# Float32r scores in the later batches, a short MAX8 for the 32nd score, and masks by VectorE alone

## The chip, the cores and the metric

The kernel runs on one core of a Trainium2 chip. The metric is the device time of one execution in microseconds. A core has five engines with a queue each: TensorE (PE in the profile), VectorE (DVE), ScalarE (ACT), GpSimd (POOL) and SyncE (SP, which issues the transfers between memory and on-chip memory). Each works through its queue in order; semaphores order work between them.

## The reference

Three stages follow one another. The first is attention over 4 batches of 8 heads, 576 positions, width 64, in which only the 32 largest scores of a row count:

```python
scores = scale * np.matmul(q, k.transpose(0, 1, 3, 2))
kth = np.partition(scores, -top_k, axis=-1)[..., -top_k:-top_k + 1]
mask = scores >= kth
scores = np.where(mask, scores, -1000000000.0)
scores = scores - np.max(scores, axis=-1, keepdims=True)
attn = np.exp(scores)
attn = attn / (np.sum(attn, axis=-1, keepdims=True) + 1e-09)
return np.matmul(attn, v).astype(np.float32)
```

The second is a dense layer on the 2304 tokens of width 512, `(x @ w_a) * (x @ w_b) @ w_out` with inner width 1536. The third picks one of 8 experts for each token (the largest of 8 logits) and computes `gate * relu(x @ w1[e]) @ w2[e]` with inner width 1024.

## The kernel before, in words

All work is written as operations with an engine, a planned cost, a position and the tiles that they read and write (`Plan.op`). `Plan.emit` plays the operations through a model of the engines, always taking the ready operation with the lowest position, and writes each engine's queue in the order that comes out. So a changed cost or a new operation can change the order of everything. Once written, the queues are fixed.

**Attention** works on units: a batch and a pair of heads. Batch 0 is cut into two halves by rows, so it has 8 half units (0 to 7); batches 1 to 3 have 4 whole units each (8 to 19). `load_unit` fetches k, q and v; `prep_unit` transposes k and q on TensorE into the buffer tp in PSUM (L473, L476), and ScalarE copies them out to kT and qT (L488). A unit's rows are cut into tiles of 128 rows of one head, taken in pairs of two heads ("N"), and one mixed tile of 64 rows of both heads ("M"). There are 144 tiles, 36 a batch.

For a pair, TensorE computes the scores in float32 in two halves of 288 columns (L533; the mixed tile L518). ScalarE copies them to the tile s (L537). VectorE forms, for each column and its partner in the other half, the larger (m) and the smaller (n) of the two scores (L544 and L545). Then it finds the 32nd largest: four rounds of MAX8 on m (L556, L572), which give the 32 largest of m in sorted order, with MATCH_REPLACE8 between them (L569), and one MAX8 on n (L575). `attn_kth` merges the two lists with a minimum of sorted ranks 24 to 31 against the eight of n in reverse order (L585) and a maximum (L587). After the first MAX8 GpSimd makes the negative maximum nm (L559) and ScalarE the exponentials e (L564).

`attn_out` masks a tile in one of two ways, which `masked(i)` picks by the tile's number: in batches 0 and 1 three tiles of four, in batches 2 and 3 one of three, 78 in all, take the split way. There VectorE compares s with the 32nd score (L609), GpSimd multiplies the result by e (L611), and ScalarE sums the row (L612). The other 66 take one fused VectorE instruction that compares, multiplies and sums (L615). TensorE transposes the masked tile (L640, L649; mixed L623 to L625), ScalarE copies it out (L644, L651), and TensorE multiplies by v (L661, L665). `attn_norm` divides by the sums.

**Around it.** In batch 0 the weights of the dense layer are converted: 36 pieces pass through ScalarE, VectorE (L383, L386), GpSimd (L389, L395) and back to memory. The dense layer of a batch (`moe1`: L758, and L788 for w_out) runs in float32r with each operand split into a high and a low part. Its matmuls have the lowest priority of all, so they fill TensorE between the steps of the next batch's attention. Its weights come in through a buffer of three (L736, L776) by the SP queue, as do the loads of k, q and v. After attention follow the dense layer of batch 3 and the experts (`expert`, L1033 to L1238).

The lines that carry the choice of the mask:

```python
if masked(i):
    P(DVE, c_ts(S), pos, lambda: nc.vector.tensor_scalar(am(), sc(), kth(), None, op0=OP.is_ge), ...)
    P(POOL, c_pool(S), pos, lambda: nc.gpsimd.tensor_mul(am(), am(), e()), r=[e], w=[amk])
    P(ACT, c_act(S, True) + 90, pos, lambda: nc.scalar.activation(
        e(), am(), AF.Copy, accum_out=r.sum()[:, j:j + 1]), r=[amk], w=[e, (r.sum, j)])
else:
    P(DVE, c_dve(S) + 60, pos, lambda: nc.vector.scalar_tensor_tensor(
        am(), sc(), kth(), e(), op0=OP.is_ge, op1=OP.mult, accum_out=r.sum()[:, j:j + 1]), ...)
```

## Time and profile before

| | |
|---|---|
| median of 3 runs | 1248.7 us (1246.32 to 1249.34) |
| profiled execution | 1250.73 us, its span 1248.9 us |
| mean granted TensorE clock | 0.944 |
| TensorE busy | 1136.4 us (91% of the span) |
| VectorE busy | 893.8 us (72%) |
| ScalarE busy | 741.5 us (59%) |
| GpSimd busy | 539.2 us (43%) |

The shares are means over stages that differ much: VectorE works almost without a break up to about 805 us and little after that. The end of a matmul is modelled, so a busy TensorE can still have short gaps. The first masks fall at 22 us; attention ends at about 818 us.

### The profile page before, as it was taken

To read this page: it belongs to the slowest core of one execution; us is meant where nothing else is said; L and a number is where in the kernel's file an instruction comes from. 1 tells how busy PE (TensorE), PEld (TensorE's weight loads), DVE (VectorE), ACT (ScalarE), POOL (GpSimd) and SP (SyncE) were. 2 spreads that over 40 slices of the span, in tenths; PEclk is the share of its full clock that TensorE was granted. 3 is DMA by queue.
4 is the path that set the end of the run, shared out by engine and by line. 5 is a ranking of instruction groups with operands and counts; after the bars stand their busy time and mean duration, and the time that the engine had idled before them with its cause. 6 is when DMAs were issued, how large, how long until landed. Compare 5 with 4: busy or idle time off the path is not lost.

```text
span 1248.9 us, 22260 instructions
## 1 busy us (share of the span) xinstructions
PE 1136.4 (91%) x7614; PEld 950.9 (76%) x7614; DVE 893.8 (72%) x2574; ACT 741.5 (59%) x1639; POOL 539.2 (43%) x673
## 2 busy tenths in 40 slices
PE   5666587987999999999999999999899999999997
PEld 2333365675687878878878777899899889999996
DVE  6999989999989999989999898901004644444451
ACT  6767677777677776656766665633223545544451
POOL 4766667577554744324544532555334110000011
PEclk9966588898899999999999999999999999999999
DMA  7486566898466554243243322345545645554550
GB/s 232 137 275 186 164 178 188 288 327 264 161 208 200 188 183 131 77 130 131 77 137 100 113 86 104 119 140 202 196 167 179 200 151 171 181 175 145 166 180 28
DMA packets 133375, 208.01 MB, mean 167 GB/s; under 512 B 53075, under 2 KB 95059, under 8 KB 125573
## 3 DMA queue, kind: packets, MB, share of 16 engines
q1 hardware_dynamic: 130037, 197.04, 48.5%
q0 software_dynamic: 3216, 9.46, 2.0%
q8 instruction: 62, 1.02, 0.3%
q14 instruction: 60, 0.49, 0.1%
HBM read 171.82 MB, written 35.25 MB: 166 GB/s over the span
## 4 chain that ended last, share of the span: by engine, by line
PE 62%; DVE 20%; issue 7%; DMA 5%; ACT 3%; POOL 2%; SPq 1%; POOLq 0%; ACTq 0%; DVEq 0%
PE ab L758 20%; PE ab L788 11%; PE sp L533 5%; PE ab L1116 5%; DVE m L569 4%; PE pv L661 4%; DVE kt L572 4%; PE tp L640 3%; PE ms L1165 3%; PE pv L1165 3%; DVE am L609 2%; DVE kt L556 1%; DMA xsort<-rows,pi 1%; DVE am L615 1%; DVE m L545 1%
## 5 line engine op out<-in xcount | busy, mean ns | idle before, releaser
L758 PE MATMUL ab<-xh,wt 128*128 128x320 f32 (+1 forms) x1344 | 311.1, 309 | 3.4 <-ACT sb L743 3.4
L758 PEld LDWEIGHTS ab<-xh,wt 128*128 128x128 f32 x1344 | 228.3, 192 | 30.3 <-issue 22.6
L758 PE MATMUL ab<-xl,wt 128*128 128x320 f32 (+1 forms) x672 | 200.4, 298 | 0.0
L569 DVE MATCH_REPLACE8 m<-kt,m 128x288 f32<-128x288 f32 x432 | 190.6, 447 | 0.0
L572 DVE MAX8 kt<-m 128x8 f32<-128x288 f32 x432 | 184.8, 452 | 0.7
L788 PE MATMUL ab<-gH,wt 128*128 128x320 f32 (+1 forms) x768 | 172.0, 307 | 2.8 <-DMA wt<-wos 2.8
L533 PE MATMUL sp<-kT,qT 64*128 64x288 f32 x512 | 111.2, 514 | 40.5 <-ACT s L537 13.0
L766 POOL TENSOR_TENSOR sa<-sa,sb 128x320 f32<-128x320 f32 (+1 forms) x96 | 80.2, 836 | 149.2 <-ACT sb L743 145.6
L788 PEld LDWEIGHTS ab<-gH,wt 128*128 128x128 f32 x768 | 129.8, 193 | 14.9 <-issue 10.1
L611 POOL TENSOR_TENSOR am<-am,e 128x576 f32<-128x576 f32 x78 | 119.1, 1532 | 31.8 <-DVE am L609 25.7
L758 PEld LDWEIGHTS ab<-xl,wt 128*128 128x128 f32 x672 | 129.2, 192 | 0.0
L1190 POOL DMA_INDIRECT out_dram<-y,ti x23 | 23.0, 999 | 228.0 <-ACT y L1184 213.3
L564 ACT ACTIVATE e<-s,nm 128x576 f32<-128x576 f32 x144 | 109.5, 777 | 16.4 <-POOL nm L559 15.5
L788 PE MATMUL ab<-gT,wt 128*128 128x320 f32 (+1 forms) x384 | 114.8, 299 | 0.0
L640 PE MATMUL tp<-idr,am 128*128 128x128 f32 x512 | 87.9, 307 | 24.7 <-DVE am L615 12.3
L1034 DVE TENSOR_TENSOR wp<-raw,wp 128x1024 fp32r<-128x1024 f32 (+1 forms) x73 | 67.5, 943 | 55.0 <-ACT wp L1033 52.6
L537 ACT COPY s<-sp 128x576 f32<-128x576 f32 x128 | 81.8, 639 | 41.9 <-PE sp L533 31.0
L395 POOL TENSOR_TENSOR gT<-sa,gH 128x320 fp32r<-128x320 f32 (+1 forms) x96 | 82.6, 861 | 39.5 <-ACT gH L394 38.1
L640 PEld LDWEIGHTS tp<-idr,am 128*128 128x128 f32 x512 | 65.7, 157 | 44.4 <-POOL am L611 14.4
L533 PEld LDWEIGHTS sp<-kT,qT 64*128 64x128 f32 x512 | 44.1, 209 | 72.3 <-issue 28.2
L1116 PE MATMUL ab<-xgh,wp 128*128 128x304 f32 (+6 forms) x352 | 89.5, 312 | 1.2 <-DVE gT L1123 0.7
L644 ACT COPY aT<-tp 128x512 f32<-128x512 f32 x128 | 73.4, 586 | 24.6 <-PE tp L640 23.7
(286 smaller groups left out, 2559.6 us busy)
## 6 DMA issues: line engine op xcount, KB each, us to landing
wt<-ws SPq DMA_DIRECT2D x54, 1024.0 KB, 4.8
wt<-wos SPq DMA_DIRECT2D x44, 768.0 KB, 4.6
raw<-in_moe_w_dram SPq DMA_DIRECT2D x64, 512.0 KB, 3.5
xsort<-rows SPq DMA_DIRECT2D x8, 771.0 KB, 10.5
wp<-ws SPq DMA_DIRECT2D x6, 1024.0 KB
rawk<-in_k_dram SPq DMA_DIRECT2D x40, 128.0 KB, 3.6
vt<-in_v_dram SPq DMA_DIRECT2D x20, 256.0 KB, 4.4
gT<-in_moe_w_a_dram SPq DMA_DIRECT2D x8, 512.0 KB
```

The lines of the kernel that those rows point to most:

```text
L395: P(POOL, c_pool(cost), pos, lambda: nc.gpsimd.tensor_sub(lo(), src(), fr(hi())), r=rd + wh, w=wl)
L533: res = nc.tensor.matmul(sp()[:, h, 0:HS], u.qT()[a, c * 128:(c + 1) * 128], u.kT()[a, k0 + hf * HS:k0 + (hf + 1) * HS], start=True, stop= ...
L537: P(ACT, c_act(S), pos, lambda hf=hf, sp=sp: nc.scalar.copy(s()[:, :, hf * HS:(hf + 1) * HS], sp()[:, :, 0:HS]), r=[sp], w=[(s, (h, hf)) f ...
L564: P(ACT, c_act(S, True) + 90, pos, lambda h=h, e=e: nc.scalar.activation(e(), s()[:, h], AF.Exp, bias=nm()[:, h], scale=SCALE), r=[(s, (h, ...
L569: P(DVE, c_dve(HS), pos + 5.0 * h, lambda x=x, h=h, j=j: nc.vector.match_replace(out=m()[:, h], in_to_replace=kt(j, 8 * x - 8, 8 * x), in_ ...
L572: P(DVE, c_dve(HS), pos + 5.0 * h, lambda x=x, h=h, j=j: nc.vector.max(out=kt(j, 8 * x, 8 * x + 8), in_=m()[:, h]), r=[(m, h)], w=[KT(j, x)])
L611: P(POOL, c_pool(S), pos, lambda: nc.gpsimd.tensor_mul(am(), am(), e()), r=[e], w=[amk])
L640: res = nc.tensor.transpose(tp()[:, 512 * h + x * 128:512 * h + (x + 1) * 128], z()[:, 640 * h + x * 128:640 * h + (x + 1) * 128], idf)
L758: res = nc.tensor.matmul(pa()[:, 0:n], view()[:, m, wi, ko, :], xv()[:, ko], start=(ko == 0 and x == 0), stop=(ko == KO - 1 and x == 2))
L766: P(POOL, c_pool(n), pos, lambda: nc.gpsimd.tensor_mul(sa()[:, 0:n], sa()[:, 0:n], sb()[:, 0:n]), r=[sb], w=[sa])
L788: res = nc.tensor.matmul(pa()[:, 0:n], wv()[:, wi, f, :], gv()[:, f, :], start=(f == 0 and x == 0), stop=(f == HB - 1 and x == 2))
L1116: res = nc.tensor.matmul(pa()[:, 0:cap], p1[ko]()[:, wi, f * 128:(f + 1) * 128], xv()[:, ko], start=(ko == 0 and i == 0), stop=(ko == KO - ...
```

## The change

There are four edits. Units 8 to 19 (batches 1 to 3) compute their scores in float32r: k and q are split into a high part (ScalarE) and a low part (GpSimd), laid side by side in `hl`, and transposed together, so that the contraction runs over 128 rows, high and low. A second copy of kT with the two halves of its rows swapped (kS) is made by two transfers on the SP queue, and each score half is the sum of a product with kT and one with kS. Units 0 to 7 keep the float32 way (`u.f`, the list FU). The merge of the 32nd score becomes one MAX8 over 16 numbers for each tile. `masked` is false for every tile, so all 144 take the fused instruction. In the mixed tile one transpose grows from 64 × 64 to 128 × 128, over a part of the mask buffer that is set to zero once. The planned costs of the float32 score change from 510 to 780.

```diff
+    FU = opts.get("fu", range(8))
...
-    am_t = [cst.tile([128, S], F32, name="am0")]
+    am_t = [cst.tile([128, 640], F32, name="am0")]
...
+    nc.gpsimd.memset(am_t[0][:, S:640], 0.0)
...
+    for i in range(2):
+        qm_t.append(cst.tile([128, 192], F32R, name=f"qm{i}"))
+        nc.gpsimd.memset(fr(qm_t[i]), 0.0)
...
+            load(c_dma(262144), pos, lambda z=z: z()[:, 0:8, :].rearrange("p (h c) d -> p h c d", h=2),
+                 src[b, h0:h0 + 2, 0:512, :].rearrange("h (p c) d -> p h c d", c=4), [(z, 0)])
             for h in range(2):
+                load(c_dma(16384), pos, lambda z=z, h=h: z()[64 * h:64 * h + 64, 8, :], src[b, h0 + h, 512:576, :],
+                     [(z, 1 + h)])
...
+        u.kS = T(p_at, [128, 2, 640], F32R, "kS", opts.get("kS", 2))
+        for ni, nm in enumerate(("k", "q")):
             raw = u.raw[nm]
+            p0 = pos + 3 * ni * step
+            hl = T(p_at, [128, 9, 2, 64], F32R, "hl", opts.get("hl", 1))
+            P(ACT, c_act(576, True), p0, lambda raw=raw, hl=hl: nc.scalar.copy(hl()[:, :, 0, :], raw()[:, 0:9, :]),
+              r=[raw], w=[(hl, 0)])
+            P(POOL, c_pool(576), p0, lambda raw=raw, hl=hl: nc.gpsimd.tensor_sub(
+                hl()[:, :, 1, :], raw()[:, 0:9, :], fr(hl()[:, :, 0, :])), r=[raw, (hl, 0)], w=[(hl, 1)])
+            for h in range(2):
+                p1 = p0 + step * (1 + h)
+                t = T(p_ps, [128, 1024], F32R, "tp", 1)
+                lst = [(c, 4 * h + c) for c in range(4)] + ([(4, 8)] if h else [])
+
+                def tr(t=t, lst=lst, hl=hl):
+                    for c, j in lst:
+                        r = nc.tensor.transpose(t()[:, c * 128:(c + 1) * 128],
+                                                hl()[:, j].rearrange("p a d -> p (a d)"), idr)
+                    return r
+                P(PE, 56 * len(lst), p1, tr, r=[hl], w=[t], act=0)
...
+                    for a in range(2):
+                        u.mark = P(SP, c_dma(294912), p1, lambda a=a: nc.sync.dma_start(
+                            fr(u.kS()[64 * a:64 * a + 64]).rearrange("p h c -> p (h c)")[:, 64:],
+                            fr(u.kT()[64 - 64 * a:128 - 64 * a]).rearrange("p h c -> p (h c)")[:, 64:]),
+                          r=[u.kT], w=[(u.kS, a)])
...
+                        for x, kk in enumerate((u.kT(), u.kS())):
+                            res = nc.tensor.matmul(sp()[:, h, 0:HS], u.qT()[:, h, c * 128:(c + 1) * 128], kk[:, h, kc],
+                                                   start=(x == 0), stop=(x == 1))
...
-        P(DVE, 77 + 8 * (j1 - j0 - 1), pos, lambda: nc.vector.tensor_tensor(
-            kt(32, 40), r.kt()[:, j0:j1, 30:22:-1], kt(40, 48), op=OP.min), r=KT(2) + KT(3) + KT(5), w=KT(4))
-        P(DVE, 78 + 9 * (j1 - j0 - 1), pos, lambda: nc.vector.tensor_reduce(
-            r.kth()[:, j0:j1], kt(31, 40), axis=AX.X, op=OP.max), r=KT(3) + KT(4), w=[(r.kth, j) for j in range(j0, j1)])
...
+        for j in range(j0, j1):
+            P(DVE, 80, pos, lambda j=j: nc.vector.max(out=r.kt()[:, j, 40:48], in_=r.kt()[:, j, 24:40]),
+              r=[(r.kt, (j, 3)), (r.kt, (j, 4))], w=[(r.kt, (j, 5))])
...
-                nc.tensor.transpose(tp()[0:64, 512:576], am()[0:64, 512:S], idf[0:64, 0:64])
...
+                nc.tensor.transpose(tp()[:, 512:640], amz()[:, 512:640], idf)
...
-        return any(a <= i < b and i % m < n for a, b, n, m in opts.get("mk", ((0, 72, 3, 4), (72, 144, 1, 3))))
+        return any(a <= i < b and i % m < n for a, b, n, m in opts.get("mk", ()))
```

## Rows read from the trace of the kernel before

**Rows 1.** Busy us by stretch: PE, PEld, DVE, ACT, POOL, PE clock, DMA, GB/s.

```profile
0.00:245.00 245.00, 165.92 (x781) 107.22 (x781) 229.03 (x605) 173.99 (x374) 160.51 (x177) 0.78 0.67 205
245.00:355.00 110.00, 97.02 (x607) 73.02 (x604) 104.41 (x319) 80.38 (x183) 68.27 (x75) 0.92 0.77 246
355.00:810.00 455.00, 452.61 (x3278) 365.77 (x3277) 415.15 (x1358) 304.75 (x709) 212.37 (x292) 1.00 0.39 130
810.00:1249.00 439.00, 420.89 (x2956) 404.86 (x2954) 145.18 (x296) 182.39 (x374) 98.05 (x130) 0.99 0.49 163
```

**Rows 2.** The chain that ended last, around the end of attention: start, us, what.

```profile
811.52 0.87 PE tp L640 x8
...
818.39 7.11 PE ab L758 x54
825.50 19.20 PE ab L788 x144
```

**Rows 3.** Groups by line, VectorE, 0 to 355 us: busy us, mean ns, idle before.

```profile
L609 DVE TENSOR_SCALAR am<-s,kth 128x576 f32<-128x576 f32 x42 | 29.5, 726 | 0.1
L556 DVE MAX8 kt<-m 128x8 f32<-128x288 f32 x58 | 25.7, 452 | 0.0
...
L615 DVE SCALAR_TENSOR_TENSOR am<-s,kth,e 128x576 f32<-128x576 f32 x14 | 16.9, 1209 | 0.0
...
L585 DVE TENSOR_TENSOR kt<-kt 128x16 f32<-128x16 f32 (+1 forms) x31 | 11.0, 354 | 0.1
...
L587 DVE TENSOR_REDUCE kth<-kt 128x2 f32<-128x18 f32 (+1 forms) x31 | 4.9, 159 | 0.1
...
L615 DVE DVE_READ_ACCUMULATOR am<-s,kth,e 128x1 f32 x14 | 1.1, 80 | 0.0
```

**Rows 4.** Single instructions in order of time, VectorE and GpSimd: start, us, what.

```profile
264.79 1.40 POOL L611 TENSOR_TENSOR am<-am,e 128x576 f32<-128x576 f32 x1
...
264.95 1.85 DVE L615 SCALAR_TENSOR_TENSOR am<-s,kth,e 128x576 f32<-128x576 f32 x1
...
272.08 0.42 DVE L383 TENSOR_SCALAR x<-x 128x512 int32<-128x512 int32 x1
...
273.99 0.68 DVE L386 SCALAR_TENSOR_TENSOR x<-xl,x 128x512 int32<-128x512 int32 x1
...
314.02 0.79 DVE L615 SCALAR_TENSOR_TENSOR am<-s,kth,e 128x576 f32<-128x576 f32 x1
...
314.75 0.51 DVE L609 TENSOR_SCALAR am<-s,kth 128x576 f32<-128x576 f32 x1
```

**Rows 5.** VectorE busy by stretch for L386 alone, then for L383 alone.

```profile
0.00:355.00 355.00, 38.82 (x36) 0.82 0.70 218
...
0.00:355.00 355.00, 25.51 (x36) 0.82 0.70 218
```

**Rows 6.** Groups by line, GpSimd, 0 to 355 us.

```profile
L611 POOL TENSOR_TENSOR am<-am,e 128x576 f32<-128x576 f32 x42 | 65.0, 1556 | 15.2 <-DVE am L609 15.0
```

**Rows 7.** Single instructions in order of time, TensorE, around one half score.

```profile
500.74 0.76 PE L533 MATMUL sp<-kT,qT 64*128 64x288 f32 x4
501.42 0.66 PE L640 MATMUL tp<-idr,am 128*128 128x128 f32 x4
```

**Rows 8.** Line L640: what TensorE's idle time before it waited for, us, times.

```profile
  DVE am L615: 25.9, 13
  POOL am L611: 19.5, 25
  ACT qT L488: 9.1, 6
```

**Rows 9.** Groups by line, TensorE, 355 to 810 us.

```profile
L640 PE MATMUL tp<-idr,am 128*128 128x128 f32 x308 | 45.3, 275 | 0.5 <-ACT aT L644 0.2
```

**Rows 10.** Waits of the SP queue: us in total, times, longest us.

```profile
SPq L776 <- PE ab L758: 170.2, 21, 16.2
```

**Rows 11.** Transfers by line: count, KB each, median us to landing.

```profile
vt<-in_v_dram SPq DMA_DIRECT2D x20, 256.0 KB, 4.4
```

More of the change, by code (lines that the diff above doesn't have):

```diff
@@ L323, in fused_kernel @@
         nc.gpsimd.memset(gb_t[i], 0.0)
+    QM = [P_.fixed(t) for t in qm_t]
     RR = [P_.fixed(t) for t in rr_t]
@@ L427, in load_unit @@
         u = Rec()
-        u.b, u.p, u.first = b, p, ui == 0
+        u.b, u.p, u.f, u.first = b, p, ui in FU, ui == 0
         ch = [x - x // 3 for g in groups for x in GT[g] if x != 2]
@@ new lines, in prep_unit, with tr, out @@
+        u.qm, u.rr = QM[i % 2], RR[i % len(RR)]
+        u.qT = T(p_at, [128, 2, 512], F32R, "qT", 2)
+        u.kT = T(p_at, [128, 2, 640], F32R, "kT", 2)
+        if u.f:
+            u.qv, u.kv = (lambda z=z: fr(z()).rearrange("p h c -> p (h c)")[:, 0:640] for z in (u.qT, u.kT))
+            for ni, (nm, z, dst) in enumerate((("k", u.kT, u.kv), ("q", u.qT, u.qv))):
+                raw = u.raw[nm]
+                p1 = pos + 3 * ni * step
+                a, e, last = u.c if nm == "q" else (0, 4, True)
+                t = T(p_ps, [128, 512], F32, "pv", 1) if u.first and nm == "q" else T(p_ps, [128, 1024], F32, "tp", 1)
+                cut = [(a, e, last)] if not u.first or nm == "q" else [(0, 2, False), (2, 4, True)]
+                for a, e, last in cut:
+                    o = 128 * e if u.first and nm == "q" else 512
+                    def tr(t=t, raw=raw, a=a, e=e, last=last, o=o):
+                        for c in range(a, e):
+                            res = nc.tensor.transpose(t()[:, c * 128:(c + 1) * 128],
+                                                      raw()[:, 2 * c:2 * c + 2, :].rearrange("p a d -> p (a d)"), idf)
+                        if last:
+                            res = nc.tensor.transpose(t()[:, o:o + 64], raw()[0:64, 8:10, :].rearrange("p a d -> p (a d)"),
+                                                      idf[0:64, 0:64])
+                        return res
+                    P(PE, 110 * (e - a) + 60 * last, p1, tr, r=[raw], w=[(t, a)], act=0)
+                    def out(t=t, dst=dst, a=a, e=e, last=last, o=o, f=64 * (nm == "k")):
+                        if last and f:
+                            nc.scalar.copy(dst()[:, 0:64], t()[:, 512:S])
+                        if last and 128 * e < 512:
+                            nc.scalar.copy(dst()[:, 512:S], t()[:, o:o + 64])
+                            last = False
+                        x, y = 128 * a, S if last else 128 * e
+                        return nc.scalar.copy(dst()[:, f + x:f + y], t()[:, x:y])
+                    u.mark = P(ACT, c_act(128 * (e - a) + 64 * last) + (150 if last and (e < 4 or nm == "k") else 0), p1,
+                               out, r=[(t, a)], w=[(z, a)])
+            return
@@ L495, in new_group @@
         r.kt = T(p_sml, [128, 5, 48], F32, "kt", 2)
-        r.kth = T(p_sml, [128, 5], F32, "kth", 2)
         r.sum = T(p_sml, [128, 5], F32, "sum", 2)
@@ L515, in score @@
             def score():
-                for hh, hf in ((0, 0), (1, 1), (0, 1), (1, 0)):
-                    a = slice(64 * hh, 64 * hh + 64)
-                    res = nc.tensor.matmul(sp()[a, hf, 0:HS], u.qT()[a, 512:576], u.kT()[a, 64 + hf * HS:64 + (hf + 1) * HS],
-                                           start=True, stop=True)
-                return res
-            P(PE, 980, pos, score, r=[u.qT, u.kT], w=[sp], label=f"score{u.b}")
+                if u.f:
+                    for hh, hf in ((0, 0), (1, 1), (0, 1), (1, 0)):
+                        a = slice(64 * hh, 64 * hh + 64)
+                        res = nc.tensor.matmul(sp()[a, hf, 0:HS], u.qv()[a, 512:576],
+                                               u.kv()[a, 64 + hf * HS:64 + (hf + 1) * HS], start=True, stop=True)
+                    return res
+                for hf in range(2):
+                    for hh in range(2):
+                        for kk in (u.kT(), u.kS()):
+                            res = nc.tensor.matmul(sp()[:, hf, 0:HS], u.qm()[:, 64 * hh:64 * hh + 128],
+                                                   kk[:, hh, 64 + hf * HS:64 + (hf + 1) * HS],
+                                                   start=(hh == 0 and kk is u.kT()), stop=(hh == 1 and kk is u.kS()))
+                return res
+            P(PE, 980 if u.f else c_mm(HS, 8), pos, score, r=[u.qT, u.kT] if u.f else [u.qm, u.kT, u.kS], w=[sp],
+              label=f"score{u.b}")
             P(ACT, c_act(S), pos, lambda: nc.scalar.copy(
```

92 lines of the change are left out of this document (40 added, 52 removed).

## The prediction

> **What bounds the kernel now.** I read the busy time by stretch first, then the costs of the mask and 32nd-score instructions in the first stretch, then single instructions in order of time, then what TensorE and the transfer queue wait for. The stretches [rows 1] show two regimes. Up to 355 us VectorE is busy 229.0 of 245 and 104.4 of 110 us, while TensorE has gaps and a granted clock of 0.78 and 0.92. From 355 us to the end of attention near 810 us TensorE is busy 452.6 of 455 us at clock 1.00, and it stays near full after that. So there are two prices. A microsecond that VectorE gains or loses before 355 us moves everything behind it. After 355 us the order is set by the sum of TensorE's work, because the low-priority matmuls of the dense layers fill whatever attention leaves. VectorE idles 39.8 us of that stretch, and when the last attention matmul is done 7.1 + 19.2 = 26.3 us of the older batch's filler is still to run [rows 2]. Lengthening attention there is therefore hidden up to about 26 us, while TensorE work counts in full.
>
> **VectorE in the first 355 us.** 56 tiles are masked there: 42 with the short comparison plus a GpSimd product, 14 with the fused instruction [rows 3]. The change turns the 42 into fused ones.
>
> Removed: 42 × 0.726 = 30.5 us of comparisons. Added: 42 fused instructions. The nearest row is the fused instruction of the same stretch, 1.209 us, and its accumulator read of 0.080 us: 42 × 1.289 = 54.1 us. The 31 pairs of minimum and reduction cost 11.0 + 4.9 = 15.9 us. In their place come 56 MAX8 over 16 numbers. No row shows one; it lies between the reduction over 18 numbers or fewer (0.159) and MAX8 over 288 (0.452), and I take 0.16, from the row nearest in size: 9.0 us. At 0.452 it would be 25.3 us. Without any further effect VectorE gains 54.1 − 30.5 − 15.9 + 9.0 = +16.7 us.
>
> Against this stands contention. Alone, a fused instruction takes 0.79 us and a comparison 0.51; one that starts while a GpSimd product runs took 1.85 us and ended 0.61 us after that product [rows 4]. The two conversion instructions at L386 and L383 take 38.8 and 25.5 us for 36 each [rows 5] where their undelayed rows say 0.68 and 0.42 [rows 4]: 14.3 + 10.4 = 24.7 us of delay. The products are 65.0 of GpSimd's 228.8 us in this stretch [rows 1, 6], 28%. I credit the conversion with that share, 7.0 us, and leave the fused instructions at their row, since 56 of them instead of 14 now meet the rest of GpSimd's work. That gives +9.7 us. The ends: +16.7 with no relief; and with every fused instruction at its undelayed 0.79 us, 42 × 0.87 − 30.5 − 14 × 0.419 − 6.9 − 7.0 = −13.7 us. I stay nearer the upper end because the only fused instructions measured in this stretch have that mean.
>
> The Trainium skill's page "SBUF — State Buffer", section "Who interferes with whom", says that VectorE and GpSimd share one port pair as an exclusive lock, taken by VectorE instructions with two SBUF inputs and by the two-port modes of tensor_scalar. The 1.85 us row agrees. If that is all there is to the delays, removing products removes whole blocks, and MAX8, with one input, cannot be blocked at all: the sum would move towards the −13.7 end, which the faster rival below takes from rows.
>
> After 355 us the same swap is at most 36 × (1.289 − 0.726) = 20 us; it hides in the 39.8 us that VectorE idles and in the 26.3 us of filler. If that cover were gone it would be paid.
>
> **GpSimd and ScalarE.** The products and the ScalarE sums go. Twelve later units gain two GpSimd subtractions and two ScalarE copies each for the high and low parts, and more copies out of PSUM. GpSimd was busy 212.4 and ScalarE 304.8 of 455 us, so I cost them at nothing. The fused instruction now also waits for the exponential, which a comparison did not; behind it VectorE's whole queue would stand. The exponential is issued after the first of four MAX8 rounds, so three rounds cover it.
>
> **TensorE after 355 us.** A pair's half score is four instructions of 0.68 us in all (500.74 to 501.42) [rows 7]. The float32r version is four matmuls of 288 columns. The 144 filler matmuls, half of them 320 and half 256 columns wide, take 19.20 us [rows 2], 0.133 each: 0.533 us. Eight halves a unit save 1.18 us. The mixed tile keeps eight instructions, and I leave it even. Preparing a unit now takes eight full transposes and two narrow ones; the float32r path takes 18 full ones. No row shows a float32r transpose. The nearest is the float32 one, 0.87 us for eight, 0.109 each [rows 2]: 1.96 us instead of about 0.98 (narrow ones at half). The wider mixed-tile transpose adds 0.05. Over 12 units: 12 × (−1.18 + 0.98 + 0.05) = −1.8 us. At half the price of the row it is −13.6 us, at twice +21.7 us. The sum takes −1.8.
>
> **New waits.** Preparing a unit becomes a chain: loads, ScalarE copy, GpSimd subtraction, then four trips from TensorE to ScalarE through the single buffer tp instead of two, then two copies of kT into kS on the SP queue. TensorE now waits 9.1 us in all behind the copies of the last trip (L488) [rows 8], 0.46 us for each of 20 units. Two more trips a unit and the kS transfer, in 12 units of which the first two or three lie before 355 us, give 12 × 2 × 0.46 = 11 us if nothing covers them; TensorE has filler to run between trips, and its transposes wait only 0.5 us after 355 us [rows 9], so I take 4 us. The ends are 0 and 18 us, the upper one if a third of a landing like vt's 4.4 us [rows 11] is bare in each unit. Behind a waiting kS transfer on SP stand weight loads. One of those holds the queue for 170.2 / 21 = 8.1 us on average today [rows 10], and kS can stand behind it as well.
>
> TensorE waits 19.5 us in 25 waits behind products, but 25.9 us in 13 behind fused instructions [rows 8]. I cost the removal of the first at nothing: before 355 us VectorE's queue sets the pace, and a shorter wait for GpSimd becomes a wait for VectorE.
>
> The small set-up fills on GpSimd cost nothing; it idles over a third of the first stretch.
>
> **The sum.** +9.7 − 1.8 + 4 = +11.9 us on the profiled execution's 1250.7 us (span 1248.9 and 1.8 around it): 1262.6. The median of the runs, 1248.7, is 2.0 lower, so I predict 1260.6, rounded to 1260.5.
>
> **Rivals.** *The port comes free (faster).* The delays are all blocks by GpSimd and the removed products take them along. For it: the 1.85 us row. Against: conversion work fills the room. Price: −13.7 on VectorE, other terms kept, −13.7 − 1.8 + 4 = −11.5, 1237 us. It decides once the fused instructions of the first stretch fall below 1.209 − 11.9 / 42 = 0.93 us on average. Chance 0.27. This is the way in which the lock that the Trainium skill's page "SBUF — State Buffer" describes would work here.
>
> *The terms cancel.* The relief lands about halfway, fused instructions near 0.93 us: 1249 us. Chance 0.13.
>
> *Float32r transposes cost twice the float32 row* (or kS comes late in every unit, about as dear). TensorE then has 21.7 instead of −1.8: 1284 us. For it: no row has the shape. Against: the float32r filler takes 0.133 us for 288 columns, which is 0.059 for 128. Chance 0.10.
>
> *My forecast*: 0.50, with a range of its own from 1252 to 1270 (VectorE +3 to +16.7, waits 0 to 8, rounded).
>
> The 8-in-10 range is 1237 to 1280: it leaves out half of the faster rival and most of the third. A measurement of this kernel tells 0.3%, some 3.7 us, from no change. Faster 0.27, same 0.13, slower 0.60.
>
> **What would show it.** In the profile after: the fused instruction's mean in the first stretch (1.2 us, or below 0.93); the time at which TensorE becomes full (about 10 us later than 355, or earlier); L386 and L383 delays of 18 us, not 25 or 10; the price of a float32r transpose, start to start, beside 0.109 us; TensorE's idle time before scores and transposes in the later batches; the time by which the short MAX8 differs from 0.16 us. The prediction is wrong if VectorE is done with the first 56 tiles no later than now, or if TensorE has gaps of several us a unit after 355 us.

## The result, and the profile after

| | before | after |
|---|---|---|
| median of the runs | 1247.9 us (4 runs) | 1233.4 us (1231.7 to 1235.9, 4 runs) |
| profiled execution's span | 1248.9 us | 1231.4 us |
| mean granted TensorE clock | 0.944 | 0.956 |

The ratio is 0.9882, with a 95% interval of 0.9866 to 0.9898: the changed kernel is 1.2% faster. The forecast was 1260.5 us, with a range from 1237 to 1280. Both the sign and the range were wrong.

Percentages of whole kernels below are ratios of their runs to runs of the kernel before on the same chip; 1% is 12.5 us.

The stretches of the changed kernel, in the columns of [rows 1] (the last one ends with the span, at 1231.4 us):

```profile
0.00:245.00 245.00, 169.91 (x893) 117.64 (x894) 229.22 (x660) 170.72 (x353) 137.79 (x167) 0.85 0.77 233
245.00:355.00 110.00, 98.19 (x730) 87.32 (x728) 103.65 (x331) 77.06 (x177) 57.98 (x77) 0.97 0.86 273
355.00:810.00 455.00, 433.54 (x3290) 389.31 (x3289) 419.94 (x1357) 296.97 (x690) 181.61 (x269) 0.99 0.40 130
810.00:1249.00 439.00, 401.94 (x2804) 386.92 (x2802) 143.51 (x291) 173.35 (x349) 83.17 (x110) 0.98 0.48 158
```

Two things differ from [rows 1]. TensorE does more in the first 355 us (1623 matmul records instead of 1388, at a higher granted clock). And from 355 to 810 us it is idle for 455 − 433.5 = 21.5 us, where it was 2.4 before.

VectorE's groups of the mask and of the 32nd score, 0 to 355 us, answer to [rows 3]:

```profile
L680 DVE SCALAR_TENSOR_TENSOR am<-s,kt,e 128x576 f32<-128x576 f32 x58 | 58.7, 1029 | 0.1
L652 DVE MAX8 kt<-kt 128x8 f32<-128x16 f32 x58 | 8.2, 161 | 0.0
L680 DVE DVE_READ_ACCUMULATOR am<-s,kt,e 128x1 f32 x58 | 4.5, 78 | 0.0
```

The conversion lines, L386 and L383 before and L392 and L389 now, as in [rows 5]:

```profile
0.00:355.00 355.00, 29.18 (x36) 0.88 0.80 245
...
0.00:355.00 355.00, 21.17 (x36) 0.88 0.80 245
```

The fused instruction takes 1.03 us, not 1.21. The conversion takes 50.3 us, not 64.3. For the same 56 tiles VectorE's account is: masks 56 × (1.029 + 0.078) − 42 × 0.726 − 14 × 1.289 = +13.5 us, 32nd score 9.0 − 15.9 = −6.9, conversion −14.0: in all −7.4 us. The 56th mask ends at 341.7 us, where it ended at 348.9 before, so the account holds within 1 us.

More than those 7 us is gained on TensorE. Its filler, the dense layer of batch 0, starts at 147.3 instead of 160.1 us, and by 355 us 642 of its matmuls have started, 474 before. At the 0.133 us of [rows 2] the 168 more are 22.3 us of TensorE's later work. Two things that the filler needs come sooner: attention of batch 0 (36 masks) ends at 230.1 instead of 237.9 us, and VectorE's last conversion instruction at 269 instead of 297 us. No run separates what each of them gives.

Part of it is given back around 400 to 450 us. TensorE's busy time there, its count, granted clock, DMA share and GB/s, in the kernel before:

```profile
400.00:450.00 50.00, 50.00 (x382) 1.00 0.67 228
```

and in the changed one:

```profile
400.00:450.00 50.00, 38.23 (x254) 0.90 0.34 110
```

Single instructions of the changed kernel there, in order of time, show what is missing (start, us, what, idle time before it and what ended it):

```profile
420.26 0.31 PE L824 MATMUL ab<-xl,wt 128*128 128x320 f32 x1
420.41 0.31 PE L824 MATMUL ab<-xh,wt 128*128 128x320 f32 x1
423.53 0.37 PE L601 MATMUL sp<-kT,qT 128*128 128x288 f32 x1 [2.81 <-DVE kt L652]
...
425.33 1.02 PE L706 MATMUL tp<-idr,am 128*128 128x128 f32 x4 [1.04 <-DVE am L680]
...
437.46 0.53 PE L523 MATMUL tp<-idr,hl 128*128 128x128 f32 x4 [1.97 <-POOL hl L514]
437.83 0.35 PE L824 MATMUL ab<-xh,wt 128*128 128x256 f32 x1
```

Between 420.4 and 437.8 us no filler (L824, L854) runs. The dense layer of batch 0 is used up (its 864 matmuls have started by 402.2 us). Of batch 1's, 24 matmuls of the first 320 rows run up to 420.4 us; the next in the queue have to wait for batch 1's attention, whose last mask ends at 426.0 us. In the kernel before, the filler of batch 0 lasts until attention is through, and there is no such pause.

At the end of attention, on the chain of waits, there is again filler left of the older batch, as in [rows 2]:

```profile
807.79 3.23 PE ab L854 x24
811.02 0.22 PE pv L769 x2
811.24 13.51 PE ab L854 x102
```

### The profile page after: what moved, and what is told of

Read it like the earlier page. It is cut to its first block, busy times and chain, and to the rows that moved or that the text cites. A ratio compares the mean times of both kernels' runs of the same rounds, so it can differ in the third digit from the quotient of the medians.

```text
span 1231.4 us, 22514 instructions
## 1 busy us (share of the span) xinstructions
PE 1103.6 (90%) x7710; PEld 981.2 (80%) x7710; DVE 896.3 (73%) x2636; ACT 718.1 (58%) x1567; POOL 460.6 (37%) x622
## 3 DMA queue, kind: packets, MB, share of 16 engines
q8 instruction: 63, 1.03, 0.4%
## 4 chain that ended last, share of the span: by engine, by line
PE 55%; DVE 14%; DMA 11%; issue 8%; ACT 7%; POOL 4%; SPq 1%; POOLq 0%; ACTq 0%; DVEq 0%
PE ab L824 16%; PE ab L854 9%; PE ab L1182 5%; PE pv L727 5%; DVE am L680 3%; DVE m L638 3%; PE ms L1231 3%; PE pv L1231 3%; PE sp L601 3%; DVE kt L641 2%; PE tp L706 2%; DMA xsort<-rows,pi 2%; DMA rawk<-in_k_dram 2%; DMA wt<-wos 1%; PE pv L731 1%
## 5 line engine op out<-in xcount | busy, mean ns | idle before, releaser
L824 PE MATMUL ab<-xh,wt 128*128 128x320 f32 (+1 forms) x1344 | 303.9, 304 | 3.9 <-ACT sb L809 3.8
L824 PEld LDWEIGHTS ab<-xh,wt 128*128 128x128 f32 x1344 | 227.6, 191 | 13.2 <-issue 7.8
L824 PE MATMUL ab<-xl,wt 128*128 128x320 f32 (+1 forms) x672 | 199.9, 297 | 0.0
L641 DVE MAX8 kt<-m 128x8 f32<-128x288 f32 x432 | 182.3, 444 | 0.5
L854 PE MATMUL ab<-gH,wt 128*128 128x320 f32 (+1 forms) x768 | 171.8, 305 | 4.5 <-DMA wt<-wos 4.5
L680 DVE SCALAR_TENSOR_TENSOR am<-s,kt,e 128x576 f32<-128x576 f32 x144 | 139.8, 996 | 0.3
L854 PEld LDWEIGHTS ab<-gH,wt 128*128 128x128 f32 x768 | 130.7, 193 | 6.7 <-DMA wt<-wos 3.9
L824 PEld LDWEIGHTS ab<-xl,wt 128*128 128x128 f32 x672 | 128.8, 192 | 0.0
L854 PE MATMUL ab<-gT,wt 128*128 128x320 f32 (+1 forms) x384 | 115.1, 300 | 0.0
L1100 DVE TENSOR_TENSOR wp<-raw,wp 128x1024 fp32r<-128x1024 f32 (+1 forms) x73 | 67.4, 942 | 55.6 <-ACT wp L1099 55.2
L706 PE MATMUL tp<-idr,am 128*128 128x128 f32 x512 | 84.8, 304 | 20.3 <-ACT aT L710 7.2
L401 POOL TENSOR_TENSOR gT<-sa,gH 128x320 fp32r<-128x320 f32 (+1 forms) x96 | 84.6, 881 | 45.8 <-ACT gH L400 45.4
L706 PEld LDWEIGHTS tp<-idr,am 128*128 128x128 f32 x512 | 64.1, 155 | 38.6 <-ACT aT L710 15.8
L710 ACT COPY aT<-tp 128x512 f32<-128x512 f32 x128 | 72.4, 587 | 26.6 <-PE tp L706 25.8
L727 PE MATMUL pv<-aT,vt 128*64 128x320 f32 (+1 forms) x512 | 79.2, 451 | 6.5 <-ACT aT L695 4.5
L809 ACT ACTIVATE sa<-ab 128x320 f32<-128x320 f32 (+1 forms) x120 | 49.4, 412 | 53.9 <-PE ab L824 30.7
```

The lines of the kernel that those rows point to most:

```text
L401: P(POOL, c_pool(cost), pos, lambda: nc.gpsimd.tensor_sub(lo(), src(), fr(hi())), r=rd + wh, w=wl)
L641: P(DVE, c_dve(HS), pos + 5.0 * h, lambda x=x, h=h, j=j: nc.vector.max(out=kt(j, 8 * x, 8 * x + 8), in_=m()[:, h]), r=[(m, h)], w=[KT(j, x)])
L706: res = nc.tensor.transpose(tp()[:, 512 * h + x * 128:512 * h + (x + 1) * 128], z()[:, 640 * h + x * 128:640 * h + (x + 1) * 128], idf)
L727: nc.tensor.matmul(pv()[64 * h:64 * h + 64, 0:n], u.vt()[:, h, j, :], r.aT[h]()[:, j, 0:n], start=(j == 0), stop=False)
L824: res = nc.tensor.matmul(pa()[:, 0:n], view()[:, m, wi, ko, :], xv()[:, ko], start=(ko == 0 and x == 0), stop=(ko == KO - 1 and x == 2))
L854: res = nc.tensor.matmul(pa()[:, 0:n], wv()[:, wi, f, :], gv()[:, f, :], start=(f == 0 and x == 0), stop=(f == HB - 1 and x == 2))
```

## The experiments

Theory A is that the gain comes from VectorE in the first stretch: fewer and shorter instructions there, and above all fewer that stand still while GpSimd holds the path to on-chip memory; for float32r it counts TensorE's saved work in full. Theory B is that the gain comes from TensorE's waits behind the products, theory C that it comes from the changed order of the queues. The conditions of each are in the expectations. For float32r, theory F1 is that GpSimd's subtractions delay VectorE later on, F2 that the longer preparation delays TensorE, and F3 that TensorE's saving meets a stretch without filler in batch 1. The diffs are against the kernel before where it says so, else against the changed one. After each time stands the ratio to the kernel before.

**Masks alone** (kernel before).

```diff
-        ... for a, b, n, m in opts.get("mk", ((0, 72, 3, 4), (72, 144, 1, 3))))
+        ... for a, b, n, m in opts.get("mk", ()))
```

> The kernel before with the fused mask on all 144 tiles and nothing else changed. Theory A (the GpSimd products delayed VectorE by holding what they share, and that goes): fused instructions in the first 355 us fall to 1.03 us, the conversion lines L386 and L383 lose 14 us of delay, which pays for the longer masks (42 x 0.38 = 16 us), so 1246 to 1250 us. Theory B (TensorE's waits behind products were the price, so the gain of the whole change is here): 1236 to 1240 us. Forecast on record (longer masks are paid): 1255 to 1265 us.

Measured: 1236.5 us, 0.9898 (0.9863 to 0.9933). Fused 1.040 us, conversion 45.6 us, 36th mask at 227.2 us. Against the forecast, fused instructions for every tile are by themselves worth 1%. The time lies in theory B's range; the signs on VectorE are theory A's, with 18.7 us of relief on the conversion instead of 14. This run alone does not decide between the two.

**Short MAX8 alone** (kernel before).

```diff
-        P(DVE, ..., nc.vector.tensor_tensor(kt(32, 40), r.kt()[:, j0:j1, 30:22:-1], kt(40, 48), op=OP.min), ...)
-        P(DVE, ..., nc.vector.tensor_reduce(r.kth()[:, j0:j1], kt(31, 40), axis=AX.X, op=OP.max), ...)
...
+        for j in range(j0, j1):
+            P(DVE, 80, ..., nc.vector.max(out=r.kt()[:, j, 40:48], in_=r.kt()[:, j, 24:40]), ...)
```

> The kernel before with one MAX8 over 16 numbers a tile instead of the minimum and the reduction a pair. Theory A: VectorE saves 15.9 - 9.0 = 6.9 us before 355 us and nothing counts after, so 1240 to 1243 us. Theory B: nothing, 1246 to 1250 us.

Measured: 1238.8 us, 0.9914 (0.9891 to 0.9936). MAX8 over 16 numbers takes 0.160 us. The gain is somewhat larger than theory A's; theory B, which gave it nothing, falls here. The conversion stays at 64.7 us, but the fused instruction falls from 1.209 to 1.041 us and the comparison from 0.726 to 0.670, with the same products on GpSimd.

**Float32r alone** (the changed kernel with the split masks and the two-instruction 32nd score put back).

```diff
-        ... opts.get("mk", ()))
+        ... opts.get("mk", ((0, 72, 3, 4), (72, 144, 1, 3))))
...
-            P(DVE, 80, ..., nc.vector.max(out=r.kt()[:, j, 40:48], in_=r.kt()[:, j, 24:40]), ...)
+        P(DVE, ..., nc.vector.tensor_tensor(..., op=OP.min), ...)
+        P(DVE, ..., nc.vector.tensor_reduce(..., op=OP.max), ...)
```

> The kernel before with the float32r scores of units 8 to 19 (and the changed loads, mixed transpose and planned costs that come with them), split masks and minimum with reduction kept. Theory A (TensorE's work after 355 us counts in full): with 0.53 us a half score and 0.085 us a transpose, 12 x 0.58 = 7 us less, 1239 to 1243 us. Theory B: under 3 us, 1245 to 1250 us.

Measured: 1247.5 us, 0.9988 (0.9973 to 1.0004). No gain, as theory B had it; the 7 us of TensorE's work on which theory A counted do not show in the time.

**Masks and MAX8 without float32r.**

```diff
-    FU = opts.get("fu", range(8))
+    FU = opts.get("fu", range(20))
```

> The changed kernel with float32 scores in all 20 units, so masks, MAX8, the mixed transpose and the planned costs remain. Theory A: it loses the 7 us of TensorE work, 1239 to 1242 us. Theory B (waits behind products carry the gain): within 3 us of the changed kernel, 1233 to 1237 us.

Measured: 1234.8 us, 0.9874 (0.9852 to 0.9895): the same as the whole change. The time is again in theory B's range, and not in theory A's. Float32r in twelve units is worth nothing in the sum. The two other parts give 1.02% and 0.86% alone and 1.26% together, less than their sum; whether they draw on the same delays is not shown, since each also changes the order of the queues.

**The planned cost alone** (kernel before).

```diff
-                P(PE, 510, pos, score, ...)
+                P(PE, 780, pos, score, ...)
```

> The kernel before with the planned cost of a float32 half score raised from 510 to 780, which changes the order of the queues and no instruction. Theory C (the changed order gives the gain): 1232 to 1240 us. Theories A and B: 1245 to 1252 us.

Measured: 1246.9 us, 0.9992 (0.9973 to 1.001). The order that the new cost writes gains nothing, so theory C falls for this cost. Two rows of this run bear on what follows. The 56th mask ends at 338.5 us, 10.4 us sooner than in the kernel before and with the same instructions, but only 516 filler matmuls have started by 355 us (474 before): masks that end early are not by themselves worth their microseconds. And the fused instruction, with every product in place, takes 1.054 us from 0 to 355 us:

```profile
L615 DVE SCALAR_TENSOR_TENSOR am<-s,kth,e 128x576 f32<-128x576 f32 x14 | 14.8, 1054 | 0.0
```

**The split masks without the product** (kernel before).

```diff
-            P(POOL, c_pool(S), pos, lambda: nc.gpsimd.tensor_mul(am(), am(), e()), r=[e], w=[amk])
```

> The kernel before without the 78 GpSimd products; it leaves out the multiplication by the exponentials in those tiles, so the masks themselves are transposed and summed. VectorE keeps every instruction. Theory A (GpSimd's products make VectorE wait): the conversion lines L386 and L383 lose 12 to 19 us of delay in the first 355 us, the 36th mask ends at 220 to 228 us instead of 238, 1225 to 1235 us. Theory B (TensorE's waits behind products): 1230 to 1240 us, but with VectorE's instructions as long as before and the 36th mask at 235 to 238 us.

Measured: 1240.5 us, 0.9929 (0.9902 to 0.9955). Taking only the products away, with comparisons and ScalarE sums kept, gives 0.7 of the 1.0% of all fused masks. Conversion 47.5 us, 36th mask at 226.0 us, both as theory A had them; fused 1.010 us. But the comparison is dearer (0.832 us instead of 0.726), and the time lies just above both ranges.

**GpSimd work put back, with nothing that needs it.** Two versions of the kernel without float32r, each with an unused GpSimd instruction behind the same 78 masks: a multiplication that reads two tiles, and a fill of 1600 columns that only writes.

```diff
-            P(DVE, c_dve(S) + 60, pos, lambda: nc.vector.scalar_tensor_tensor(
+            st = P(DVE, c_dve(S) + 60, pos, lambda: nc.vector.scalar_tensor_tensor(
...
+                P(POOL, ..., lambda: nc.gpsimd.tensor_mul(scr[:, 0:S], scr[:, S:2 * S], scr[:, S:2 * S]), ...).deps.add(st)
```

> The changed kernel with float32 scores in all units (e4), and after each of the 78 fused masks that were split before one GpSimd multiplication of 576 constants that nobody reads. No instruction waits for it except GpSimd's own queue. Theory A: VectorE's delays come back, L386 and L383 together above 58 us instead of 48.5, fused instructions above 1.15 us, the 36th mask at 238 us or later, 1244 to 1256 us. Theory B: nothing on TensorE's path waits for a product, so 1233 to 1238 us.

```diff
+                P(POOL, ..., lambda: nc.gpsimd.memset(scr, 0.0), ...).deps.add(st)
```

> As e10, but the 78 extra GpSimd instructions are fills of 1600 numbers, of about the product's length, that read nothing. Theory A, if reading is what blocks VectorE's instructions with two inputs: fused instructions stay at 1.03 us and 1233 to 1240 us. If GpSimd's time alone were the matter (the small products nm come late behind it): as e10, 1244 us or more.

Measured: 1242.1 us, 0.9945 (0.9925 to 0.9966), and 1243.0 us, 0.9955 (0.9937 to 0.9974), against 0.9874 without. Groups by line, 0 to 355 us, first the kernel without float32r (with the conversion line L389 by stretch below it; in the two versions the same line is L392, and L392 is L395):

```profile
L680 DVE SCALAR_TENSOR_TENSOR am<-s,kt,e 128x576 f32<-128x576 f32 x59 | 60.0, 1033 | 0.1
...
0.00:355.00 355.00, 20.88 (x36) 0.84 0.76 235
```

then with the multiplications:

```profile
L687 POOL TENSOR_TENSOR scr<-scr 128x576 f32<-128x576 f32 x42 | 55.1, 1313 | 0.6
...
0.00:355.00 355.00, 25.07 (x36) 0.87 0.74 227
...
L683 DVE SCALAR_TENSOR_TENSOR am<-s,kt,e 128x576 f32<-128x576 f32 x58 | 62.4, 1092 | 1.2 <-ACT e L636 1.2
```

and with the fills:

```profile
L687 POOL MEMSET scr<- 128x1600 f32 x42 | 60.9, 1450 | 0.4
...
0.00:355.00 355.00, 34.94 (x36) 0.87 0.72 224
L683 DVE SCALAR_TENSOR_TENSOR am<-s,kt,e 128x576 f32<-128x576 f32 x56 | 52.6, 956 | 2.8 <-ACT e L636 2.8
```

The multiplications lengthen all three of VectorE's kinds: the fused instruction by 0.06 us, L389 by 4.2 us and L392 by 3.0 us in all. The fills do not lengthen the fused instruction (0.956 us), but they take L389, with its one input, from 0.58 to 0.97 us. Single instructions show it too. First, with multiplications, a fused instruction that starts inside one; then, with fills, the line L389 and a fused instruction that start inside one:

```profile
244.33 1.36 POOL L687 TENSOR_TENSOR scr<-scr 128x576 f32<-128x576 f32 x1
244.60 1.71 DVE L683 SCALAR_TENSOR_TENSOR am<-s,kt,e 128x576 f32<-128x576 f32 x1
...
214.87 1.43 POOL L687 MEMSET scr<- 128x1600 f32 x1
215.48 1.10 DVE L392 TENSOR_SCALAR x<-x 128x512 int32<-128x512 int32 x1
...
237.82 1.43 POOL L687 MEMSET scr<- 128x1600 f32 x1
238.48 0.81 DVE L683 SCALAR_TENSOR_TENSOR am<-s,kt,e 128x576 f32<-128x576 f32 x1
```

All eight fused instructions that start inside a fill take 0.80 to 0.82 us; the nine that start inside a multiplication take 1.02 to 1.71. The Trainium skill's page "SBUF — State Buffer", section "Who interferes with whom", says that an instruction of VectorE with two on-chip inputs meets only those of GpSimd that read, while tensor_scalar in its two-port mode takes the whole shared pair. The first half agrees with these numbers; so does the second if L389 runs in that mode, which no run here shows by itself.

Nothing on TensorE's path waits for the unused multiplications, so theory B (1233 to 1238 us) fails here; that TensorE's waits behind the products carry some of the remaining gain is not excluded. Theory A's signs came in part: conversion 55.6 us instead of above 58, fused 1.09 instead of above 1.15, 36th mask at 236.0 us (229.4 without) instead of 238 or later. The fills were forecast at 1233 to 1240 us, because the forecast saw the fused instruction and not L389; they cost as much as the multiplications.

**The changed kernel without the short MAX8** (minimum and reduction put back, masks all fused).

> The changed kernel with the minimum and reduction a pair in place of the short MAX8. Theory A (VectorE's own length before 355 us and its blocks): the minimum has two inputs and is blocked again, about 5 us before the 56th mask, 1236 to 1241 us. If masks alone carry all: 1232 to 1236 us.

Measured: 1245.2 us, 0.9972 (0.9956 to 0.9988), slower than theory A forecast. VectorE's groups, 0 to 355 us:

```profile
L685 DVE SCALAR_TENSOR_TENSOR am<-s,kth,e 128x576 f32<-128x576 f32 x56 | 61.6, 1132 | 0.1
L655 DVE TENSOR_TENSOR kt<-kt 128x16 f32<-128x16 f32 (+1 forms) x31 | 10.5, 338 | 0.1
```

The 31 pairs cost 15.2 us where MAX8 costs 9.0, and the fused instruction is 0.10 us longer, 5.8 us over 56. That is 12.0 us more, and the conversion gives back 2.4 (47.9 us). The 56th mask ends 11.0 us later than in the changed kernel, and by the ratios the time is 11.2 us longer. So the size fits, but that the fused instruction would be dearer was not foreseen. It also means that the parts do not add: masks alone gain 1.0%, masks with float32r 0.3%. Why that order of the queues meets GpSimd more often stays open.

**The low parts by ScalarE.** GpSimd's subtractions are replaced by ScalarE copies; the run leaves out the low parts, so its scores are not those of the reference.

```diff
-            P(POOL, c_pool(576), p0, lambda ...: nc.gpsimd.tensor_sub(
-                hl()[:, :, 1, :], raw()[:, 0:9, :], fr(hl()[:, :, 0, :])), r=[raw, (hl, 0)], w=[(hl, 1)])
+            P(ACT, c_act(576, True), p0, lambda ...: nc.scalar.copy(hl()[:, :, 1, :], raw()[:, 0:9, :]),
+              r=[raw], w=[(hl, 1)])
```

> The changed kernel with the 24 GpSimd subtractions of the low parts left out: ScalarE writes the high part a second time in their place, so the scores are not those of the reference. Theory F1 (float32r's gain on TensorE is lost because its GpSimd work blocks VectorE): fused instructions after 355 us fall from 0.974 to about 0.88 us, the 72nd mask ends near 419 us instead of 426, 1224 to 1230 us. Theory F2 (it is lost in the longer chain of preparation): TensorE's gaps between 355 and 500 us stay at 15 us, 1232 to 1236 us.

Measured: 1229.9 us, 0.9836 (0.9812 to 0.9859), 0.46% better than the change. The fused instruction after 355 us falls from 0.974 to 0.924 us (0.870 with no float32r). The time is what theory F1 forecast, its path is not: the 72nd mask ends at 434.1 us, later than the changed kernel's 426.0, where F1 put it near 419, and the last mask ends later too (805.1 against 801.9 us), with only 30 more filler matmuls done by then. So the 24 subtractions, 1.48 us each, may have a price, but on which path it is paid is not shown, and an order of the queues alone can move the time as much (the planned costs below).

**Float32 kept in batch 1 too.**

```diff
-    FU = opts.get("fu", range(8))
+    FU = opts.get("fu", range(12))
```

> The changed kernel with float32 scores in batch 1 too; float32r remains in units 12 to 19 only. Theory F3 (in batch 1 TensorE has no use for the time it saves, since the filler of batch 0 is used up before batch 1's attention ends; in batches 2 and 3 it has): 1228 to 1232 us. If float32r is worth nothing anywhere: 1233 to 1236 us.

Measured: 1226.4 us, 0.9814 (0.9791 to 0.9837): faster than both kernels, by 0.68% against the change, and below theory F3's range.

**Planned costs near the measured ones** (kernel without float32r).

```diff
-                P(PE, 780 ..., pos, score, ...)
+                P(PE, 690 ..., pos, score, ...)
...
-            P(DVE, 80, pos, ... nc.vector.max(...)
+            P(DVE, 160, pos, ... nc.vector.max(...)
...
-            P(DVE, c_dve(S) + 60, pos, ... nc.vector.scalar_tensor_tensor(
+            P(DVE, 1080, pos, ... nc.vector.scalar_tensor_tensor(
```

> e4 (float32 scores everywhere) with planned costs near the measured ones: fused mask 1080, short MAX8 160, half score 690. No instruction changes. If the order of the queues still leaves waits: 1228 to 1233 us. If not, as e4: 1233 to 1237 us.

Measured: 1238.5 us, 0.9919 (0.9898 to 0.994), against 0.9874 without and above both ranges: truer costs made a worse order. No instruction differs, so the order alone moved the time by 0.45%. A difference of that size between two kernels whose queues differ says little about one instruction.

**Float32r in batch 1 alone, and in batch 3 alone.**

```diff
-    FU = opts.get("fu", range(8))
+    FU = opts.get("fu", list(range(8)) + list(range(12, 20)))
```

> The changed kernel with float32r scores in batch 1 alone (units 8 to 11); batches 2 and 3 go back to float32. Theory F3 (in batch 1 the filler of TensorE is used up, so that TensorE work saved there is worth nothing while the GpSimd subtractions and the longer preparation delay attention): slower than the same kernel with no float32r at all (1234.8 us), by about the 7.0 us that lie between the changed kernel (1233.4) and the one with float32 kept in batch 1 (1226.35): 1239 to 1244, and TensorE gaps between 355 and 500 us of 12 us or more, where the kernel without float32r has 3.5. Rival (the gain and the loss are not bound to a batch; float32r pays half of its whole effect anywhere): 1231 to 1235.

```diff
-    FU = opts.get("fu", range(8))
+    FU = opts.get("fu", range(16))
```

> The changed kernel with float32r scores in batch 3 alone (units 16 to 19); batches 1 and 2 keep float32. Theory F3 with equal worth of batches 2 and 3: float32r in these two together took 1234.8 to 1226.35 us, so batch 3 alone gives half of it, 1229 to 1232, with TensorE gaps between 355 and 500 us like those of the kernel without float32r (3.5 us, against 9.8 with float32r in batches 2 and 3). Rival (all that batches 2 and 3 give comes from the last batch, where no attention follows): 1225 to 1228; a rival on the other side (it comes from batch 2): 1233 to 1236.

Measured: 1242.3 us, 0.9947 (0.9926 to 0.9968), and 1225.0 us, 0.9813 (0.9784 to 0.9841). With 0.9874 for none, 0.9814 for batches 2 and 3, and 0.9882 for all three, float32r costs 9 us in batch 1, gives nothing in batch 2 and 7.6 us in batch 3. For batch 1 two pairs of kernels agree, 9.1 us here and 8.5 between the changed kernel and the one with float32 kept there. The time forecast for batch 1 alone held. Of batch 3 the rival was right: it gives everything. TensorE between 400 and 450 us, first with float32r in batch 3 alone:

```profile
400.00:450.00 50.00, 47.09 (x340) 1.00 0.44 148
```

with it in batches 2 and 3:

```profile
400.00:450.00 50.00, 41.73 (x279) 0.86 0.38 128
```

and in batch 1 alone:

```profile
400.00:450.00 50.00, 43.86 (x299) 0.97 0.31 108
```

With none it is 47.1 us. Float32r units that are worked on (batch 1) or made ready (batch 2) around the pause lengthen it; batch 3 lies far from it. But the pause is not what makes batch 1 dear. From 355 to 500 us TensorE is idle for 6.9 us with float32r in batch 1 alone, where theory F3 put 12 or more, and for 3.4 us with none; with it in batches 2 and 3 the idle time is longer, 9.7 us, in a kernel that is 7.5 us faster. What counts at the end is when the last mask ends and how much filler has been done by then. Without float32r that is 791.1 us and 2352 matmuls; in batch 3 alone 791.7 and 2425, so the 73 more are 9.7 us at 0.133 us; in batch 1 alone 797.7 and 2363, 6.6 us later for 11 more. The fused instruction after 355 us takes 0.946 us there and 0.870 without float32r, which over 86 of them has the size of those 6.6 us; but in batch 3 alone it takes 0.911 and the last mask is not late, so why batch 1 pays stays open. Over the 17 kernels measured, the span less the last mask's end, less 0.133 us for each filler matmul that reads wt and has not started by then (of 3168), lies between 329 and 336 us.

**Split masks put back in batches 2 and 3** (float32 kept in batch 1).

```diff
-        ... opts.get("mk", ()))
+        ... opts.get("mk", ((72, 144, 1, 3),)))
```

> The changed kernel with float32 kept in batch 1 (1226.35 us), and the split masks (comparison on VectorE, product on GpSimd, sum on ScalarE) put back in one tile of three of batches 2 and 3 alone, 24 tiles. Theory A (the masks gain only before 355 us, where VectorE sets the pace; after it they hide): 1224 to 1230, no change. Rival (the products block VectorE anywhere, and attention's pace in batches 2 and 3 counts): 1232 to 1236, with the last mask later than the 795.9 us of the kernel without them.

Measured: 1227.0 us, 0.9831 (0.9799 to 0.9864), against 0.9814 without them: no change. The masks' gain lies in batches 0 and 1; the tiles of batch 1 that come after 355 us were not tried by themselves.

## Why the prediction was wrong

**VectorE before 355 us: the step that failed, sized +9.7, measured −7.4 us.** This is 17.1 of the 27.1 us by which the forecast missed. The fused instruction was left at its row of 1.209 us, "since 56 of them instead of 14 now meet the rest of GpSimd's work"; it came out at 1.029, and 56 × 0.18 makes the masks 10.1 us cheaper than forecast. The row was a poor sample. Of its 14 instructions eight take 0.79 to 0.84 us; two start inside a product (1.85 and 1.90), and four inside another GpSimd instruction (1.39 to 1.84). In three kernels that keep every product and differ in the order of their queues it takes 1.041 (short MAX8 alone), 1.052 (float32r alone) and 1.054 us (planned cost alone), and the unused multiplications raise it only from 1.033 to 1.092. So most of its fall is not the products' doing.

The conversion was credited with the products' 28% share of GpSimd's busy time, 7.0 us; it got 14.0, more than half of its 24.7 us of delay. A share of busy time is not a share of delay. In the trace before, 14 of the 72 conversion instructions start inside a product, and these hold 11.4 of the 24.7 us: a product takes 1.56 us, the other 210 GpSimd instructions of the stretch 0.78 on average. Taking the products alone away brings 0.7%, with the conversion at 47.5 us; putting as many unused multiplications back costs 0.7%. The range's lower end of −13.7 had covered the value; the choice "nearer the upper end" was the error. The short MAX8 was sized right (0.161 against 0.16 us).

**What it is worth.** The forecast let a microsecond of VectorE move everything behind it by a microsecond. That failed in both directions. With the planned cost alone the 56th mask ends 10.4 us sooner, and the time does not change. In the kernel without float32r it ends 10.1 us sooner, and filler in TensorE's gaps makes more of it: 627 instead of 474 matmuls by 355 us, 153 × 0.133 = 20.3 us. Idle time from 355 to 810 us takes 4.5 us back (6.9 against 2.4), which leaves 15.8; its span is 14.9 us shorter. With the planned cost alone it is 42 matmuls, 5.6 us. What decides how much filler gets into the first stretch is not shown. The other 10.0 us of the miss lie here and in the two terms on float32r below.

**After 355 us the masks cost nothing: right.** Split masks in batches 2 and 3 change nothing.

**TensorE, sized −1.8 us, measured −19.3: mis-sized.** Summed over the starts of all matmuls from 355 us on (intervals above 0.42 us taken as 0.15), TensorE's work is 19.3 us less than without float32r. The float32r price was right: the four matmuls of a half score start 0.13 us apart, as forecast. Too little was taken for float32. From the start of a filler matmul before a half score to the start of what follows it pass 0.895 us in float32 and 0.651 in float32r behind 256 columns, 0.926 and 0.679 behind 320 (medians, 355 to 810 us): 0.245 us a half, where the forecast had 0.147. Behind a transpose it is 0.89 and 0.64; first the changed kernel, then the one without float32r, single instructions in order of time:

```profile
784.91 0.27 PE L691 MATMUL tp<-idr,am 128*128 128x128 f32 x1
784.94 0.38 PE L601 MATMUL sp<-kT,qT 128*128 128x288 f32 x1
...
785.55 0.31 PE L824 MATMUL ab<-xh,wt 128*128 128x320 f32 x1
...
441.02 0.27 PE L715 MATMUL pv<-idr,am 128*128 128x128 f32 x1
441.22 0.76 PE L597 MATMUL sp<-kT,qT 64*128 64x288 f32 x4
441.91 0.39 PE L824 MATMUL ab<-xh,wt 128*128 128x256 f32 x1
```

A float32 score, on 64 rows, starts 0.20 us behind a transpose on 128 rows, which the next such transpose follows within 0.109; [rows 7], read from the group's own start, could not show that. The Trainium skill's page "TensorEngine Tiling (Array Packing)", section "Key Properties", says that a change of tiling mode drains the engine; these rows agree.

The preparation was forecast to cost 0.98 us more a unit, and comes out about even. A float32r transpose takes 0.084 us (0.38 for five below), not 0.109. And the narrow float32 one, on 64 rows, was priced at half of 0.109; it starts 0.20 us behind the one before it and lets the next instruction start 0.20 us behind itself. So k or q takes 0.73 us in float32 and 9 × 0.084 = 0.76 in float32r. First float32, then float32r:

```profile
474.47 0.60 PE L488 MATMUL tp<-idr,rawq 128*128 128x128 f32 x4
475.00 0.27 PE L491 MATMUL tp<-idr,rawq 64*128 64x64 f32 x1
475.20 1.19 PE L572 MATMUL sp<-kT,qT 64*64 64x288 f32 x8
...
626.59 0.55 PE L523 MATMUL tp<-idr,hl 128*128 128x128 f32 x5
626.97 0.35 PE L854 MATMUL ab<-gH,wt 128*128 128x256 f32 x1
```

The mixed tile, left even, takes 0.14 us less. For the 73 half scores and nine mixed tiles from 355 to 810 us that makes 73 × 0.245 + 9 × 0.14 = 19.1 us. Another 2.0 us are the 15 filler matmuls more that ran before 355 us. What takes some 2 us back is not itemised; part of the pause runs at a lower granted clock (0.90 from 400 to 450 us).

**New waits, sized +4 us within 0 to 18: near the upper end.** By the same sum TensorE's gaps from 355 us on are 15.8 us longer than without float32r. So −19.3 and +15.8 nearly cancel, and the span differs by 2.6. The step named the wrong place: it spread the wait over all units, while most of it (11.4 of 14.6 us of idle time before 810 us) lies between 355 and 500 us, around the end of batch 1, where the filler on which "TensorE has filler to run between trips" rests is used up. Of kS there is no sign. The scores that read it and the float32r transposes, groups by line from 355 to 810 us:

```profile
L601 PE MATMUL sp<-kS,qT 128*128 128x288 f32 x148 | 41.6, 296 | 0.0
L523 PE MATMUL tp<-idr,hl 128*128 128x128 f32 x144 | 17.4, 249 | 2.0 <-POOL hl L514 2.0
```

No score waits for kS, which lands in 4.5 us, and the transposes wait once, the 1.97 us behind GpSimd's subtraction at 437.46 us, with filler behind them in the queue. Nor did kS make the weights late; the SP queue's waits answer to [rows 10]:

```profile
SPq L802 <- PE ab L824: 156.5, 22, 15.8
```

**TensorE's waits for masks, costed at nothing.** What the transposes of masked tiles (now L706) waited for, as in [rows 8]:

```profile
  ACT aT L710: 23.0, 44
  DVE am L680: 12.2, 22
  ACT qT L503: 11.0, 7
```

Behind VectorE's masks and GpSimd's products they had waited 25.9 + 19.5 = 45.4 us; behind masks they now wait 12.2. But the same view gave ScalarE's copies (L644, now L710) 3.3 us before and gives them 23.0 now: up to 19.7 of the 33.2 us may only have changed their releaser, as the step supposed. No run separates the rest from VectorE's earlier masks.

**The rivals.** "The port comes free" had the sign, and for the conversion the mechanism. That its 1237 us lie so near is in part luck: VectorE gained 7.4 us, not 13.7, and the rest came from filler, which it did not have. Its threshold of 0.93 us for the fused instruction was not reached; it divides 11.9 us by 42, though all 56 instructions change, and counts 7.0 us for the conversion. With 56 and 14.0 it would be 1.209 − 4.9 / 56 = 1.12 us, and the measured 1.029 lies below that. "Float32r transposes cost twice" is out (0.084 us).

## What to carry to other kernels

Where GpSimd works on a path that it shares with VectorE, price an instruction from single rows of the trace, with and without an overlap; a mean of 14 instructions from a stretch full of overlaps depends on the order of the queues, and is no price for another order. Where low-priority work fills an engine's gaps, count how much of it has been done at the end of the stretch: here that, with the end of the last mask, follows the time, and the end of an early mask does not. Try the same code in one stretch at a time: float32r costs 9 us in batch 1 and gives 7.6 us in batch 3, for reasons that are in part open, and keeping it out of batch 1 makes 1226.4 us of 1233.4. And where a planner writes the queues, a change of order alone can move the time by half a per cent.

## What the runs showed of the hardware that was not expected

- A GpSimd fill of 1600 columns (1.45 us), which reads nothing, lengthens VectorE's tensor_scalar over 512 columns from 0.58 to 0.97 us on average; the eight two-input instructions that start inside one keep their undelayed 0.81 us.
- A float32 matmul on 64 rows starts 0.20 us behind a transpose on 128 rows, and one on 128 rows behind a transpose on 64 rows 0.20 us too; transposes on 128 rows follow one another within 0.109. The four records of a float32 half score (two matmuls in the program) come as two pairs: the second of a pair starts 0.007 us behind the first, the next pair 0.34 us behind.
- A float32r transpose of 128 × 128 takes 0.084 us from start to start, a float32 one 0.109.
